# The last batch's sums for one product made a product earlier, and ten of VectorE's operations put into the states' tokens

## The chip, the cores and the metric

The kernel runs on one core of one Trainium2 chip. The metric is device time in microseconds. Five engines of the core appear in the profile: TensorE (PE for matmuls, PEld for the loading of the weights that a matmul holds fixed), VectorE (DVE), ScalarE (ACT), GpSimd (POOL) and SyncE (SP, which only issues DMAs here). Each engine works through its own instructions in the order in which the program writes them, and waits on semaphores for the others.

## What is computed

A cross attention between tokens and states, and then a feed-forward block on the tokens and the updated states. Everything is float32.

```python
B, H, S, Ns, D = 8, 8, 512, 32, 64          # d_model = H*D = 512, d_ff = 2048

scores = x @ state^T / sqrt(D)              # tokens read from states
a      = softmax(scores);   xread = a @ state
scores2 = state @ x^T / sqrt(D)             # states read from tokens
a2      = softmax(scores2); sread = a2 @ x
x = concat(xread, sread)                    # (8*544, 512)
h = x @ w_in                                # (4352, 2048)
g = h * sigmoid(1.702 * h)                  # "quick GELU"
out = g @ w_out                             # (4352, 512)
```

There are 8 batches of 512 tokens, and beside them 8 x 32 = 256 tokens that come from the states. The kernel treats these 256 as a last, smaller batch behind the eight.

## The kernel before

**Batches.** Batches 0 and 1 are begun in an order of their own while the weights arrive. From batch 1 on, one call of `strassen_two` (line 699) does the down projection `g @ w_out` of one batch, and the attention and the up projection of the next batch are threaded into it. The last call (batch 7) has no next batch of tokens: what is threaded into it is the preparation for the states' tokens. Then follow `up_strassen` (line 1046) for the states' up projection and `strassen` (line 549) for their down projection.

**Seven products in place of eight.** All these matrix products are done in Winograd's form of Strassen's method: both factors are cut into four quarters, sums of quarters are formed, seven products of half the size are made, and their results are added up. `strassen_two` does this with the whole down projection: its products are called P1, P2, P5, P6, P3, P7 and P4, in this order. P5, P6, P3, P7 and P4 are done by the same method once more (`lowly`, which calls `strassen_low`, line 660): each of them is seven small products of 4 x (128x128 by 128x128), which the profile shows as 8 matmuls and 8 weight loads. A small product accumulates in a PSUM bank (x, y or z), and VectorE adds the bank to what is kept (line 674). A bank that is used again for a further product must have been read first.

**The sums.** A left factor at the lower level needs four sums, each made by two VectorE operations 256 wide (line 727, `steps3` for P7, `steps4` for P4, `steps12` for P3). The sums for the right factors (weights) were made in batch 1 and are fetched from DRAM (`low_load`, line 618, and `low4_load`, line 637). One quarter of each weight matrix holds a difference in the place of the weight itself, for the lower level; `low_third` (line 656) is one 512-wide VectorE operation that turns it back. The states' down projection has one level only and needs the weights turned back: T1, T2, T3, T4 and B22.

**The states' up projection.** Its left factors are sums of the quarters of `w_in`. `sr_sums` lists twenty VectorE operations for them: 0 to 15 are 512 wide, eight for each half of the hidden units (0 to 7 the first half, 8 to 15 the second; in each half two operations each for the sums s1, s2, the difference kept in `w_in`, and s4), and 16 to 19 are 256 wide sums of the tokens. `up_strassen` then goes over four units u of hidden columns. Each unit has three groups: `begin` (products x and y), `middle` (z, x again, y again) and `end` (y and z for the last time), written in the order begin(u), end(u-1), middle(u). ScalarE copies or applies the GELU, VectorE adds (line 1074). Units 0 and 1 read the first half's sums, units 2 and 3 the second half's. The last `end`, and the sums of the down projection that go with it, are done inside `strassen`.

**The order of the work** is written out by hand. `hook(name)` is called behind products, and a dictionary says which functions are called there: "P3.4" is behind the fourth small product of P3, "run" lies between P3 and P7. The argument `own` of `lowly` does the same for the sums of the down projection itself; at one place `own` comes before the hook. In the last batch before the change, `steps3` is called between P3 and P7, and the order of the twenty operations is the table `order` near line 1269.

Of the kernel before, what the change touches and what calls it, by code (L numbers as in the profile page):

```python
# [20 lines left out]
def kernel(  # L21
# [32 lines left out]
    B, H, S, D = x.shape  # L54
    Ns = state.shape[2]
# [48 lines left out]
    T1, T2, T4 = (sums[:, i].rearrange("p (f n) -> p f n", f=HF) for i in range(3))  # L104
# [88 lines left out]
    for i, v in enumerate((8.0 * most, 8.0 * (most - least))):  # L193
        t = konst.tile([P, 1], FP32, name=f"edge_{i}")
# [410 lines left out]

    NU, QT = HF // 2, S // 2


    QF = HF // 2
    T3 = w_out[:, :HF, HN:]  # L610
    low_a, low_b = ([low[:, 3 * i + k].rearrange("p (f n) -> p f n", f=QF) for k in range(3)] for i in range(2))
# [87 lines left out]
    def strassen_two(key, dst, hooks, a4):  # L699
# [3 lines left out]
        B11, B21, B22 = w_out[:, :HF, :HN], w_out[:, HF:, :HN], w_out[:, HF:, HN:]  # L703
# [6 lines left out]
        def hook(name):  # L710
            for fn, args in hooks.get(name, ()):
                fn(*args)
# [74 lines left out]
        o, h0, h1 = low_banks()  # L787
# [6 lines left out]
        else:  # L794
# [9 lines left out]
            o, h0, h1 = low_banks()  # L804
# [24 lines left out]
        def lowly(name, left, right, kept, banks, R, own):  # L829
            def at(i):  # L830
                for fn in own.get(i, ()):
                    fn()
                hook(f"{name}.{i}")

            b11, t3, b21, b22 = halves_of(right)
            strassen_low(left, (b11, t3, b21, b22, *kept), banks, R, at)
# [4 lines left out]
        steps3, left3 = sums(y_of(0, half), (v1, v2, v4))  # L841
        steps4, left4 = sums(y_of(NU, half), (q1, q2, q4))
        own6 = {}
        if not plain:
            steps12, left12 = sums(y_of(NU, 0), r)
# [6 lines left out]
        if plain:  # L852
            for fn in steps3:
                fn()
            hook("P6")
            p3 = bank(3)
            product(p3, A_of(0, 1), B22, "P3")
            o, h0, h1 = low_banks()
            lowly("P7", left3, T3, low_b, [h0, h1, o], k3, {})
        else:  # L860
            hook("P6")
            p3 = o01
            o, h0, h1 = low_banks()
            lowly("P3", left12, B22, low_b, [h0, h1, o], p3, {1: steps12[2:3], 2: steps12[3:]})
            if key + 1 < B:
                low_load(5, 1)
            hook("run")
            for fn in steps3:
                fn()
            hook("T")  # L870
            o, h0, h1 = low_banks()
            lowly("P7", left3, T3, low_a, [o, h0, h1], k3, {k + 1: steps4[k : k + 1] for k in range(4)})
            if key + 1 < B:
                low_load(2, 0)
# [8 lines left out]
        if not plain:  # L883
            o, h0, h1 = low_banks()
# [68 lines left out]
    def up_sums(b):  # L953
# [6 lines left out]
        def rooms(step):  # L960
            if step == 0:
                t = apool.tile([P, NG, NB, Ns], FP32, tag="e1", name=f"ta_{b}").rearrange("p g i n -> p (g i n)")
                a["T"] = [t[:, QT * i : QT * (i + 1)] for i in range(4)]
            elif step == 1:
# [9 lines left out]
        def R(g, i):  # L974
            return lambda: a["aT"][:, g, QT * i : QT * (i + 1)]

# [66 lines left out]

        return steps, left, [each(v) for v in (r11, r21, r22, *ts)]

    def up_strassen(b, ntok, left, right, between=()):

        QT = ntok // 2
        b11, b21, b22, t1, t2, t3, t4 = right
        banks = {}  # L1050

        def product(u, bank, lhs, rhs, first):
            if first:
                if bank == "x":
                    banks[bank, u] = psH.tile([P, 2, QT], FP32, tag="h", name=f"upx_{b}_{u}")
                else:
                    o = bank_o[2 * (u % 2) + (bank == "z")]
                    banks[bank, u] = o[:, : 2 * QT].rearrange("p (k t) -> p k t", k=2)
            ps = banks[bank, u]
            n = len(lhs)  # L1060
            for k in range(2):
                o = 2 * P * (u % 2) + P * k
                for i in range(n):
                    nc.tensor.matmul(  # L1064
                        ps[:, k], lhs[i][:, o : o + P], rhs[i],
                        start=(first and k == 0 and i == 0), stop=(i == n - 1), skip_group_check=True,
                    )
            return ps

        def gelu(dst, src):  # L1070
            nc.scalar.activation(out=dst, in_=src, func=AF.Gelu_apprx_sigmoid)  # L1071

        def add(ps, x, dst):
            nc.vector.tensor_tensor(out=dst, in0=ps, in1=x, op=ALU.add)  # L1074


        def begin(u):
            l11, l12, l21, l22, m1, m2, m4 = left(u)
            G[b, u], G[b, NU + u] = free.pop(0), free.pop(0)
            _, c12 = quarters(b, u, ntok)  # L1080
            c21, _ = quarters(b, NU + u, ntok)
            nc.scalar.copy(c21, product(u, "x", l11, b11, True))
            add(product(u, "y", m2, t2, True), c21, c12)

        def middle(u):
            l11, l12, l21, l22, m1, m2, m4 = left(u)
            c11, c12 = quarters(b, u, ntok)
            c21, c22 = quarters(b, NU + u, ntok)
            z = product(u, "z", m1, t1, True)
            gelu(c11, product(u, "x", l12, b21, False))  # L1090
            add(product(u, "y", l21, t3, False), c21, c22)
            add(z, c22, c22)
            gelu(c22, c22)

        def end(u):
            l11, l12, l21, l22, m1, m2, m4 = left(u)
            c11, c12 = quarters(b, u, ntok)
            c21, c22 = quarters(b, NU + u, ntok)
            add(product(u, "y", l22, t4, False), c21, c21)
            gelu(c21, c21)  # L1100
            add(product(u, "z", m4, b22, False), c12, c12)
            gelu(c12, c12)
            if u:
                s12(b, u - 1, ntok)

        for u in range(NU):
            begin(u)
            if u:
                end(u - 1)
            middle(u)  # L1110
            for fn, args in between[u] if u in between else ():
                fn(*args)

        def rest():
            end(NU - 1)
            s12(b, NU - 1, ntok)
            for u in range(NU):
                s3(b, u, ntok)

        return rest  # L1120
# [84 lines left out]
    B11, B12, B21, B22 = (w_out[:, HF * i : HF * (i + 1), HN * k : HN * (k + 1)] for i in range(2) for k in range(2))  # L1205
# [41 lines left out]
    for b in range(1, B):  # L1247
        if b > 1:
            ahead = {"P1a": [(up_strassen(b, S, *parts_x(b), A[b]["sums"]), ())]}
            if b == 2:  # L1250
                ahead["P3.6"] = [(low_third, (T4,))]
        else:
            ahead = {
                "P1a": low_sums(T2, low_a)
                + [(low_keep, (2, turn_rooms[0])), (T_of, (T4, B21, T2)), (low_third, (T2,))],
                "P1b": low_sums(T3, low_b) + [(low_keep, (3, turn_rooms[1])), (low_third, (T3,))],
                "P4.7": low_sums(T1, low_b) + [(low_keep, (5, turn_rooms[1])), (low_third, (T1,)), (low_third, (B22,))],
            }
            for k, step in zip((4, 5, 6), low_sums(B22, low_a)):
                ahead[f"P7.{k}"] = [step]  # L1260
            ahead["P7.6"] += [(low_keep, (6, turn_rooms[0])), (low_load, (2, 0))]
        if b + 1 < B:
            if b > 1:
                turn_x(b + 1)
            hooks = hooks_next(b + 1)
        else:

            steps, left, right = sr_sums()
            order = (
                ("P5.6", 2), ("P6.1", 3), ("P6.2", 6), ("P6.3", 7), ("P6.4", 8), ("P3.3", 9), ("P3.4", 10), ("P3.5", 11),  # L1270
                ("P7.5", 12), ("P7.6", 13), ("P4.1", 16, 17), ("P4.5", 18, 19), ("P4.6", 14), ("P4.7", 15),
            )
            hooks = {name: [steps[i] for i in n] for name, *n in order}
            hooks["P3.6"] = [(low_third, (T1,))]
            hooks["P4.7"] += [(low_third, (t,)) for t in (T2, T3, T4, B22)]
            ahead["P1a"][:0] = [steps[i] for i in (0, 1, 4, 5)]
        for name, first in ahead.items():
            hooks[name] = first + hooks.get(name, [])
        a4 = {}

        at = hooks.setdefault("run" if b > 1 else "P3a", [])
        k = 3 if b + 1 < B else 0
        at[k:k] = [(low4_load if b > 1 else low4_make, (a4,))]
        strassen_two(b, out_of(b), hooks, a4 if b > 1 else None)
        if b + 2 < B:
            load_state(b + 2)
            load_x_squares(b + 2)
    nb = P // Ns
    strassen(
        "sr", B * Ns, lambda r, n: out_s[nb * r.start : nb * r.stop, :, n],  # L1290
        [[(up_strassen("sr", B * Ns, left, right), ())]],
    )


# [28 lines left out]
```

## Time and profile before

| quantity | value |
|---|---|
| median of 8 runs | 720.5 us (720.35 to 720.54) |
| profiled execution, its own time | 720.47 us |
| its span, first to last instruction | 718.7 us |
| mean granted TensorE clock | 0.999 |
| PE busy | 703.8 us |
| DVE busy | 586.6 us |
| ACT busy | 241.6 us |
| VectorE additions of line 1074 | 140, 88.1 us |
| P6 of the last batch begins (weights) | 636.15 us |
| P3, P7, P4 begin | 642.51, 648.81, 656.34 us |
| the states' up projection begins | 662.59 us |
| the states' down projection begins | 686.84 us |

Rows of the timeline give the start in us from the span's beginning, the duration in us, engine, line, operation, written tile and read tiles, shapes, and the count of equal instructions merged into the row; in brackets stands how long the engine had been idle and what ended that. A duration runs until the result has landed, so the next operation on an engine can start before it is over. "PEld" rows show when a product's weights begin to load, which is the clearest sign of when the product could start. In the list of waits a row gives who waited for whom, the sum in us, how often, and the longest.

### The profile page before, as it was taken

The numbers are of one execution on the slowest core, as the hardware profiler recorded it, in microseconds if no ns is written. First come the engines' busy times: TensorE is split into PE (matmuls) and PEld (weight loads), VectorE is DVE, ScalarE is ACT, GpSimd is POOL, SyncE is SP. The second block draws the span as 40 slices with busy tenths as digits, with TensorE's granted clock in tenths as the row PEclk, the third lists the DMA queues.
The fourth block names the chain that finished last, engine by engine and source line by source line (L and its number), as shares of the span: only waits on it lengthen the run. The fifth ranks groups of instructions, "written<-read, shape, count | busy, mean of one in ns | idle before, by whom it ended". The sixth has DMA issues, their size and how long they took to land.

```text
span 718.7 us, 12331 instructions
## 1 busy us (share of the span) xinstructions
PE 703.8 (98%) x4951; PEld 561.1 (78%) x4951; DVE 586.6 (82%) x1199; ACT 241.6 (34%) x467; POOL 0.8 (0%) x8
## 2 busy tenths in 40 slices
PE   7989999999999999999999999999999999999996
PEld 3433444467898799879998899889987998899995
DVE  6998899739868998699878986899789987989440
ACT  5686511024214422524233423342244215200210
POOL 0000000000000000000000000000000000000000
PEclk9999999999999999999999999999999999999999
DMA  8921246016154334405450445133432340031000
GB/s 229 363 89 55 92 148 149 2 59 160 46 176 62 59 106 162 77 1 123 156 122 0 111 141 133 18 74 125 154 50 53 110 162 15 1 115 62 17 1 29
DMA packets 104362, 68.43 MB, mean 95 GB/s; under 512 B 87665, under 2 KB 95345, under 8 KB 104305
## 3 DMA queue, kind: packets, MB, share of 16 engines
q1 hardware_dynamic: 104304, 67.65, 33.0%
q8 instruction: 39, 0.64, 0.4%
q14 instruction: 19, 0.15, 0.1%
HBM read 54.79 MB, written 12.85 MB: 94 GB/s over the span
## 4 chain that ended last, share of the span: by engine, by line
PE 88%; DVE 6%; DMA 3%; ACT 2%; issue 1%; SPq 0%; DVEq 0%; ACTq 0%
PE low L669 17%; PE o L1064 17%; PE o L720 14%; PE o L669 8%; PE o L518 7%; PE h L500 7%; PE upx L1064 6%; PE M L320 4%; PE o L561 2%; PE o L320 1%; PE sr L480 1%; PE warm L125 1%; DVE g L727 1%; DMA out_dram<-osb_sr 1%; PE eT L469 1%; DMA out_dram<-osb 1%
## 5 line engine op out<-in xcount | busy, mean ns | idle before, releaser
L1074 DVE TENSOR_TENSOR g<-o,g 128x512 f32<-128x512 f32 (+1 forms) x140 | 88.1, 650 | 55.5 <-PE o L1064 54.5
L720 PE MATMUL o<-w_out,g 128*128 128x256 f32 x480 | 107.9, 381 | 0.0
L720 PEld LDWEIGHTS o<-w_out,g 128*128 128x128 f32 x480 | 90.1, 190 | 18.4 <-issue 6.3
L1071 ACT ACTIVATE g<-g 128x512 f32<-128x512 f32 (+1 forms) x84 | 49.8, 600 | 101.9 <-DVE g L1074 101.9
L1064 PE MATMUL upx<-aT,M 128*128 128x256 f32 x192 | 49.3, 379 | 0.0
L1064 PE MATMUL o<-ta,M 128*128 128x256 f32 x192 | 49.3, 379 | 0.0
L1064 PE MATMUL o<-ta,ms 128*128 128x256 f32 x192 | 48.3, 379 | 0.0
L460 ACT COPY M<-M 128x512 f32<-128x512 f32 x64 | 33.2, 597 | 29.7 <-PE M L320 29.7
L1064 PEld LDWEIGHTS o<-ta,ms 128*128 128x128 f32 x192 | 36.5, 190 | 5.0
L1064 PEld LDWEIGHTS o<-ta,M 128*128 128x128 f32 x192 | 36.5, 190 | 5.0
L669 PE MATMUL low<-low,g 128*128 128x128 f32 x304 | 40.2, 275 | 0.0
L1064 PEld LDWEIGHTS upx<-aT,M 128*128 128x128 f32 x192 | 36.1, 190 | 4.7
L669 PEld LDWEIGHTS low<-low,g 128*128 128x128 f32 x304 | 37.0, 192 | 0.0
L669 PE MATMUL low<-sums,later 128*128 128x128 f32 x264 | 35.0, 276 | 0.1
L669 PEld LDWEIGHTS low<-sums,later 128*128 128x128 f32 x264 | 32.7, 192 | 0.7 <-DVE pu L674 0.3
L541 DVE TENSOR_TENSOR later<-g,g 128x512 f32<-128x512 f32 (+1 forms) x32 | 20.8, 650 | 14.9 <-ACT g L503 14.9
L320 PE MATMUL M<-w_in,stT 64*32 64x512 f32 x512 | 32.7, 594 | 0.2 <-ACT eT L470 0.2
L500 PE MATMUL h<-low,M 128*128 128x512 f32 x64 | 29.8, 600 | 1.5 <-DVE low L408 1.5
L500 PE MATMUL h<-aT,M 128*128 128x512 f32 x64 | 28.7, 599 | 1.4 <-ACT M L460 1.4
L518 PE MATMUL o<-w_out,g 128*128 128x512 f32 x64 | 28.7, 594 | 0.0
L669 PE MATMUL low<-w_out,g 128*128 128x128 f32 x216 | 28.5, 275 | 0.0
L518 PE MATMUL o<-w_out,sums 128*128 128x512 f32 x64 | 28.4, 594 | 0.0
(214 smaller groups left out, 1286.4 us busy)
## 6 DMA issues: line engine op xcount, KB each, us to landing
low<-low SPq DMA_DIRECT2D x34, 768.0 KB
later<-in_moe_w_out_dram SPq DMA_DIRECT2D x16, 512.0 KB
xn<-in_x_dram SPq DMA_DIRECT2D x28, 256.0 KB
w_out<-in_moe_w_in_dram SPq DMA_DIRECT2D x12, 512.0 KB
xsq<-in_x_dram SPq DMA_DIRECT2D x96, 64.0 KB
out_dram<-osb SPq DMA_DIRECT2D x18, 256.0 KB
out_dram<-later SPq DMA_DIRECT2D x14, 256.0 KB
later<-in_moe_w_in_dram SPq DMA_DIRECT2D x4, 512.0 KB
```

The costliest lines, as they stand in the source:

```text
L125: nc.tensor.matmul(ps, zeros[:, :P], zeros, start=True, stop=True)
L320: nc.tensor.matmul(ps[g][st], A[b]["stT"][rows, st], rhs(rows, j), start=True, stop=True)
L460: nc.scalar.copy(m[:, g], ps[g])
L500: nc.tensor.matmul(hps, lhs[i], rhs[i], start=(i == 0), stop=(i == n - 1))
L518: nc.tensor.matmul(ops, G[key, f // 2][:, f % 2, P * r : P * (r + 1)], w_out[:, f], start=(f == 0), stop=(f == NF - 1))
L541: nc.vector.tensor_tensor(out=s1, in0=a21, in1=a22, op=ALU.add)
L561: nc.tensor.matmul(ps[:, r], lhs[f][:, P * r : P * (r + 1)], rhs[:, f], start=(first and r == 0 and f == 0), stop=(f == HF - 1), skip_grou ...
L669: nc.tensor.matmul(ps, lhs[f], rhs[:, f], start=(first and f == 0), stop=(f == QF - 1), skip_group_check=True)
L720: nc.tensor.matmul(ps[:, r], lhs[f][:, P * r : P * (r + 1)], rhs[:, f], start=(r == 0 and f == 0), stop=(f == HF - 1), skip_group_check=True,)
L1064: nc.tensor.matmul(ps[:, k], lhs[i][:, o : o + P], rhs[i], start=(first and k == 0 and i == 0), stop=(i == n - 1), skip_group_check=True,)
L1071: nc.scalar.activation(out=dst, in_=src, func=AF.Gelu_apprx_sigmoid)
L1074: nc.vector.tensor_tensor(out=dst, in0=ps, in1=x, op=ALU.add)
```

## The change

In the last batch only, `steps3`, the sums for P7, is called within P3, one pair of operations behind each of its small products 3 to 6, and no longer between P3 and P7. Ten VectorE operations of 512 columns leave `strassen_two`: the operations 10 to 15 of `sr_sums` and the restorations of T2, T3, T4 and B22. They go into `up_strassen` as a list `beside`, from which the end of each group (`begin`, `middle`, `end`) takes one, behind the group's additions. Of the rest, operations 6 and 7 are called one hook later, 8 and 9 move from P6.4 and P3.3 to P7.5 and P7.6, and T1's restoration moves from behind P3's sixth small product to behind its seventh. The other batches are as before.

```diff
-            lowly("P3", left12, B22, low_b, [h0, h1, o], p3, {1: steps12[2:3], 2: steps12[3:]})
+            own3 = {1: steps12[2:3], 2: steps12[3:]}
+            if key + 1 == B:
+                own3.update({i + 3: steps3[i : i + 1] for i in range(4)})
+            lowly("P3", left12, B22, low_b, [h0, h1, o], p3, own3)
             if key + 1 < B:
                 low_load(5, 1)
             hook("run")
-            for fn in steps3:
-                fn()
+            if key + 1 < B:
+                for fn in steps3:
+                    fn()
             hook("T")
...
-    def up_strassen(b, ntok, left, right, between=()):
+    def up_strassen(b, ntok, left, right, between=(), beside=()):
+        beside = list(beside)
...
+        def aside():
+            if beside:
+                fn, args = beside.pop(0)
+                fn(*args)
...
         def begin(u):
...
             add(product(u, "y", m2, t2, True), c21, c12)
+            aside()
...
         def middle(u):
...
             gelu(c22, c22)
+            aside()
...
         def end(u):
...
             gelu(c12, c12)
+            aside()
             if u:
                 s12(b, u - 1, ntok)
...
             order = (
-                ("P5.6", 2), ("P6.1", 3), ("P6.2", 6), ("P6.3", 7), ("P6.4", 8), ("P3.3", 9), ("P3.4", 10), ("P3.5", 11),
-                ("P7.5", 12), ("P7.6", 13), ("P4.1", 16, 17), ("P4.5", 18, 19), ("P4.6", 14), ("P4.7", 15),
+                ("P5.6", 2), ("P6.1", 3), ("P6.3", 6), ("P6.4", 7), ("P7.5", 8), ("P7.6", 9), ("P4.1", 16, 17), ("P4.5", 18, 19),
             )
             hooks = {name: [steps[i] for i in n] for name, *n in order}
-            hooks["P3.6"] = [(low_third, (T1,))]
-            hooks["P4.7"] += [(low_third, (t,)) for t in (T2, T3, T4, B22)]
+            hooks["P3.7"] = [(low_third, (T1,))]
+            beside = steps[10:16] + [(low_third, (t,)) for t in (T2, T3, T4, B22)]
             ahead["P1a"][:0] = [steps[i] for i in (0, 1, 4, 5)]
...
-        [[(up_strassen("sr", B * Ns, left, right), ())]],
+        [[(up_strassen("sr", B * Ns, left, right, beside=beside), ())]],
```

## The prediction

> **What bounds the kernel now.** I read the page first: it says which engine carries the span and whether the clock is a topic.
>
> ```profile
> span 718.7 us, 12331 instructions
> ...
> PE 703.8 (98%) x4951; PEld 561.1 (78%) x4951; DVE 586.6 (82%) x1199; ACT 241.6 (34%) x467; POOL 0.8 (0%) x8
> ```
>
> TensorE (PE) is busy 98% of the span, and the page's row of the granted clock holds a 9 (90% or more) in each of its 40 slices. So an edit to VectorE (DVE) work pays only where TensorE is waiting for VectorE. The second view is therefore the list of waits, for TensorE alone, over the last batch and the states' tokens (625 to 720 us):
>
> ```profile
> PE o L1064 <- DVE g L1074: 0.8, 1, 0.8
> PE low L669 <- ACT pu L678: 0.5, 1, 0.5
> PE low L669 <- DVE later L674: 0.2, 1, 0.2
> ```
>
> Three waits, once each. The third view, the timeline around them, shows what VectorE was doing. First the seam from the low product P3 (with B22) to P7, then the start of the states' tokens:
>
> ```profile
> 648.81 0.97 PEld L669 LDWEIGHTS o<-w_out,g 128*128 128x128 f32 x8
> ...
> 649.33 0.75 DVE L727 TENSOR_TENSOR later<-g,g 128x256 f32<-128x256 f32 x2
> 650.00 0.75 DVE L727 TENSOR_TENSOR later<-later,g 128x256 f32<-128x256 f32 x2
> 650.06 0.27 ACT L678 COPY pu<-o 128x128 f32<-128x128 f32 x1 [4.29 <-PE o L669]
> 650.49 0.97 PEld L669 LDWEIGHTS low<-low,later 128*128 128x128 f32 x8 [0.70 <-ACT pu L678]
> ...
> 654.22 0.28 DVE L674 TENSOR_TENSOR later<-low,pu 128x128 f32<-128x128 f32 x1
> ...
> 654.56 0.97 PEld L669 LDWEIGHTS low<-w_out,later 128*128 128x128 f32 x8 [0.42 <-DVE later L674]
> ...
> 663.71 0.68 DVE L1208 TENSOR_TENSOR sums<-sums 128x512 f32<-128x512 f32 x1
> ...
> 665.52 0.69 DVE L1208 TENSOR_TENSOR w_out<-w_out 128x512 f32<-128x512 f32 x1
> 666.12 0.68 DVE L727 TENSOR_TENSOR later<-g,later 128x512 f32<-128x512 f32 x1
> ...
> 666.72 0.42 DVE L1074 TENSOR_TENSOR g<-o,g 128x256 f32<-128x256 f32 x1
> ...
> 667.19 0.97 PEld L1064 LDWEIGHTS o<-ta_sr,w_in 128*128 128x128 f32 x8 [0.95 <-DVE g L1074]
> ```
>
> A product here is 8 weight loads and 8 matmuls. P7's first needs no sums. Its second reads the sum made by the pair at 650.00: the first half of that pair ends at 650.42, the weights load at 650.49. The list names ScalarE's copy, but in P3 the like product loads at 643.40, before its copy at 643.76, so the copy is no condition. At 654.56 the sixth product waits for the addition of 654.22, late because VectorE was still making P7's and P4's sums. At 667.19 the states' second product on bank "y" (the fifth in all) waits for the addition of 666.72, which stood behind the four restorations of L1208 and the last sum of the output (L727).
>
> **How much is lost.** From 668.08 to 686.84 the weight loads of 21 successive products start 18.76 us apart: 0.893 us per product. From P6's first load (636.15) to 668.08 there are 33 products, 29.47 us at that pace, in 31.93 us: 2.46 us lost. By single steps: 0.79 at 650.49, 0.51 at 654.56, 1.03 at 667.19, 0.12 at 640.73 (P6) and 0.06 at 647.03 (P3); their sum, 2.51, agrees within 0.05.
>
> The Trainium skill, "Trainium Kernel Development and Optimization", Best Practices, says to judge TensorE by the busy share of its weight loads and not by its matmuls. By the matmul rows' idle times (0.54, 0.23, 0.76) the prize would be 1.5 us, by the weight loads' (0.70, 0.42, 0.95) 2.1 us. My sum goes by the pace, because that also counts products which are only stretched.
>
> **The change, part by part.** VectorE's prices, as start to start in a queue without gaps: 0.60 us for a 512-wide operation (663.71, 664.31, 664.91), 0.67 for a pair of 256-wide ones (649.33, 650.00), 0.20 for a 128-wide addition (648.29, 648.49), about 0.42 for a 256-wide addition from PSUM.
>
> *P6.* Steps 6 and 7 move one hook later and step 8 leaves: 0.60 less. The addition to "z" then ends near 640.4 instead of 640.67, before the sixth product's nominal 640.62. Gain 0.12.
>
> *P3.* Steps 9, 10 and 11 leave (1.80), T1's restoration moves from behind the sixth product to behind the seventh, and the four pairs of P7's sums (2.68) come in behind products 3 to 6. Walking the queue, 0.12 earlier than before: pair of hook 3 at 645.97, addition z 646.64 to 646.93, pair 646.84, addition y 647.51 to 647.80, pair 647.71, addition z 648.38 to 648.67, pair 648.58, last addition 649.25, T1's restoration 649.45 to 650.05. The sixth product wants the first of these by 646.86 and gets it at 646.98: 0.12 lost, against 0.06 before (a pair costs 0.07 more than the single operation it replaces). The seventh is ready at 647.85 against 647.87, and P7's first, which reuses the bank of the third addition, at 648.72 against 648.76: both just in time. This is the tightest place; 0.02 to 0.04 us are all the slack, so I bound it by 0.12 below and by four further 0.07 (0.4 in all) above, and take 0.12, because the pairs of 644.55 and 645.42 already ran beside P3's matmuls and the loads at the same 0.67.
>
> *P7.* Its sums are then ready before it starts: 0.79 is gone. P4's four pairs start behind T1's restoration, at 650.05, instead of 652.01; the sixth product's addition ends near 652.9, wanted at 653.24: 0.51 is gone. Steps 8 and 9 replace 12 and 13, the same size: nothing. What is late next would be a load: P7's second product reads sums of weights that SP fetches behind P6, and P4 the fetch behind it. Both issue at 642.8 and 643.2 and the DMA rows are empty from 649 us; after the change they are wanted at 649.7 and 655.9. The SP queue keeps its order; POOL has nothing here.
>
> *P4 and the handover.* Step 14, step 15 and the restorations of T2, T3, T4 and B22 leave: 6 x 0.60 = 3.6 us off the queue ahead of the output's last sum and of the first addition of the states' tokens. That addition then runs as soon as its product ends (1.2 us after the weights' start: 667.19, 668.39), 1 us before it is wanted: 1.03 is gone. The last output sum and its store on SP come some 4 us earlier, into DMA engines with little to do: nothing.
>
> *The ten operations behind the additions.* 10 x 0.60 = 6.0 us of VectorE, one behind each of the first ten groups. From 668 to 686 us VectorE is busy 7.88 of 18.00 and TensorE 18.00. A unit of seven products lasts 6.25 us; with three of these (1.8), five additions (2.1) and the sums of L541/L542 (0.8) VectorE has 4.7. Walked in order, the tightest: operation 11 ends 6.2 us after the stage's start, the next addition's product at 6.6; after that addition operation 12 delays the following one by 0.13, whose result only a GELU reads. An addition that a product waits for is done about 1 us early, so more than one 0.60 would have to stand ahead of it. Its data: steps 10 to 15 serve units 2 and 3 and are done by 13.9 us; unit 2's second product, the first reader, starts at 11.6 and needs 10 and 11 (6.2), its "m4" product at 19.6 needs 14 and 15. The restored weights are read after the four units' 25 us. Cost taken: 0; without that cover up to 6.0.
>
> *The end.* The last three stores hang on each other through one output buffer (3.45 us each), but the first starts with TensorE's product (addition at 706.26), and the store before it left 3 us earlier. So the tail moves with TensorE in full.
>
> Sum: 2.46 - 0.12 = 2.34 us. The profiled execution took 720.47 us (span 718.7 and 1.77 around it), 0.03 under the median 720.5: 718.13 on it, 718.15 on the median.
>
> **The rivals.**
> *P3 becomes VectorE's.* For: the slack of 0.02 to 0.04. Against: the same pairs beside the same matmuls. With 0.4 lost in P3 and another 0.3 passed on to P7, the gain is 1.7: 718.8. Chance 0.13.
>
> *The seam is not the sums'.* If P7's second product did wait for ScalarE's copy or for the fetch, 0.79 stays: gain 1.55, 718.95. If the handover's 1.03 stayed too: 720.0, no measurable difference. Against: the load at 643.40 ahead of its copy, the empty DMA rows. Chance 0.07, half of it with no difference.
>
> *Slower: the ten operations stand on TensorE's path in the states' tokens,* for instance because a sum written in one half of a room holds back a product that reads the other half. Price up to 6.0: 720.5 - 2.34 + 6.0 = 724.2. It decides from 0.23 us per operation, where it has eaten the 2.34. Against: in P7 the pairs of 652.01 and 652.88 wrote halves of g while products read the other halves at the 0.893 pace. Chance 0.05.
>
> *It does nothing:* the stretch is recovered and lost in the tail. Against: the tail's root is TensorE. With smaller losses of every sort adding to 1 us: 719.5. Chance 0.04.
>
> **How the numbers follow.** The forecast, 718.15, has 0.71; its own range is 717.9 (all 2.46, and 0.15 of spread) to 718.6. A measurement of this kernel tells about 0.2%, 1.44 us: faster means under 719.06. Faster: 0.71 + 0.13 + 0.035, less a little for P3 losing more = 0.86; same 0.08; slower 0.06. The range goes from 717.7 to 719.2, which takes in both faster rivals and leaves out the rest.
>
> **What would show it.** Right: no idle time before P7's second product or the states' fifth product; 636.15 to the product that was at 668.08 takes 29.6 us; L1208 and L1024 rows between the L1074 rows, with TensorE at 0.893 there. Wrong: gaps over 0.2 us ahead of P3's sixth or seventh product, or a wait of L1064 for L1024 or L1074.

## The result and the profile after

| | before | after |
|---|---|---|
| median | 720.51 us (28 runs, 720.32 to 720.86) | 718.16 us (10 runs, 717.98 to 718.28) |
| profiled execution | 720.47 us, span 718.7 | 718.06 us, span 716.3 |
| VectorE busy | 586.6 us | 586.9 us |

The ratio is 0.9967, with a 95% interval of 0.9959 to 0.9975: 2.35 us faster, where 718.15 had been forecast. VectorE does exactly the same work.

The head of the page for the changed kernel:

```profile
span 716.3 us, 12331 instructions
...
PE 703.3 (98%) x4951; PEld 560.9 (78%) x4951; DVE 586.9 (82%) x1199; ACT 241.8 (34%) x467; POOL 0.8 (0%) x8
```

The list of TensorE's waits over the same stretch, from 625 us to the end, had three rows before. Now nothing stands under its head:

```profile
core 0 of [0], span 716.3 us
engine line waited for: us in total, times, longest us
```

The timeline of the changed kernel, cut to the rows that answer to those of before. Line numbers have moved: L1064 is now L1071, L1074 is L1081, L1024 is L1029 and L1208 is L1223.

```profile
645.88 0.97 PEld L669 LDWEIGHTS low<-w_out,g 128*128 128x128 f32 x8
645.89 0.75 DVE L727 TENSOR_TENSOR later<-g,g 128x256 f32<-128x256 f32 x2
...
646.56 0.28 DVE L674 TENSOR_TENSOR later<-o,pu 128x128 f32<-128x128 f32 x1
646.76 0.75 DVE L727 TENSOR_TENSOR later<-later,g 128x256 f32<-128x256 f32 x2
646.89 0.97 PEld L669 LDWEIGHTS o<-w_out,spare_M 128*128 128x128 f32 x8
...
648.68 0.97 PEld L669 LDWEIGHTS o<-w_out,g 128*128 128x128 f32 x8
...
649.57 0.97 PEld L669 LDWEIGHTS low<-low,later 128*128 128x128 f32 x8
...
649.92 0.27 ACT L678 COPY pu<-o 128x128 f32<-128x128 f32 x1 [4.36 <-PE o L669]
...
661.89 0.69 DVE L727 TENSOR_TENSOR later<-g,later 128x512 f32<-128x512 f32 x1
...
663.35 0.42 DVE L1081 TENSOR_TENSOR g<-o,g 128x256 f32<-128x256 f32 x1 [0.77 <-PE o L1071]
663.69 0.68 DVE L1029 TENSOR_TENSOR ws<-ws,w_in 128x512 f32<-128x512 f32 x1
...
664.76 0.97 PEld L1071 LDWEIGHTS o<-ta_sr,w_in 128*128 128x128 f32 x8
```

The reader should see four things. The pairs of P7's sums (645.89, 646.76) lie between P3's additions. P7's second product loads at 649.57, one pace behind its first, and ahead of ScalarE's copy at 649.92: so it was the sums that it had waited for, and not the copy that the list of before named. The first addition of the states' tokens (663.35) now finds VectorE idle for 0.77 us, and one of the ten operations follows it. Their fifth product (664.76) no longer waits.

One loss is left: between the loads at 645.88 and 646.89 lie 1.01 us where the pace is 0.893. That is the 0.12 us of P3's sixth product. Every other of the 33 products from 636.05 to 665.65 starts within 0.02 us of the pace.

### The profile page after: what moved, and what is told of

The parts are those of the page before. It is cut to its first block, busy times and chain, and to the rows that moved or that the text cites. A ratio compares the mean times of both kernels' runs of the same rounds, so it can differ in the third digit from the quotient of the medians.

```text
span 716.3 us, 12331 instructions
## 1 busy us (share of the span) xinstructions
PE 703.3 (98%) x4951; PEld 560.9 (78%) x4951; DVE 586.9 (82%) x1199; ACT 241.8 (34%) x467; POOL 0.8 (0%) x8
## 4 chain that ended last, share of the span: by engine, by line
PE 90%; DVE 3%; DMA 3%; ACT 2%; issue 0%; SPq 0%; DVEq 0%; ACTq 0%
PE low L669 19%; PE o L1071 17%; PE o L720 14%; PE o L669 9%; PE o L518 7%; PE h L500 7%; PE upx L1071 6%; PE M L320 4%; PE o L561 2%; PE o L320 1%; PE sr L480 1%; PE warm L125 1%; PE upx_sr L1071 1%; DMA out_dram<-osb_sr 1%; PE eT L469 1%; DMA out_dram<-osb 1%
## 5 line engine op out<-in xcount | busy, mean ns | idle before, releaser
L1081 DVE TENSOR_TENSOR g<-o,g 128x512 f32<-128x512 f32 (+1 forms) x140 | 88.0, 650 | 51.4 <-PE o L1071 50.5
L1071 PE MATMUL upx<-aT,M 128*128 128x256 f32 x192 | 49.3, 379 | 0.0
L1071 PE MATMUL o<-ta,M 128*128 128x256 f32 x192 | 49.3, 379 | 0.0
L1071 PE MATMUL o<-ta,ms 128*128 128x256 f32 x192 | 48.3, 379 | 0.0
L1071 PEld LDWEIGHTS o<-ta,ms 128*128 128x128 f32 x192 | 36.5, 190 | 5.0
L1071 PEld LDWEIGHTS o<-ta,M 128*128 128x128 f32 x192 | 36.5, 190 | 5.0
L1071 PEld LDWEIGHTS upx<-aT,M 128*128 128x128 f32 x192 | 36.1, 190 | 4.7
```

The lines of the kernel that those rows point to most:

```text
L1071: nc.tensor.matmul(ps[:, k], lhs[i][:, o : o + P], rhs[i], start=(first and k == 0 and i == 0), stop=(i == n - 1), skip_group_check=True,)
```

## The experiments

In what follows "lost" is the distance between the starts of two products' weight loads less 0.893 us, the method of the prediction. The theory on trial is that TensorE loses time only where VectorE's queue, walked in order, delivers an addition or a sum late, and that the length of each delay can be had from the rows' durations.

### Each half alone

The first kernel keeps the sums within P3, and puts the ten operations back where they were:

```diff
-                ("P5.6", 2), ("P6.1", 3), ("P6.3", 6), ("P6.4", 7), ("P7.5", 8), ("P7.6", 9), ("P4.1", 16, 17), ("P4.5", 18, 19),
+                ("P5.6", 2), ("P6.1", 3), ("P6.2", 6), ("P6.3", 7), ("P6.4", 8), ("P3.3", 9), ("P3.4", 10), ("P3.5", 11),
+                ("P7.5", 12), ("P7.6", 13), ("P4.1", 16, 17), ("P4.5", 18, 19), ("P4.6", 14), ("P4.7", 15),
...
-            hooks["P3.7"] = [(low_third, (T1,))]
-            beside = steps[10:16] + [(low_third, (t,)) for t in (T2, T3, T4, B22)]
+            hooks["P3.6"] = [(low_third, (T1,))]
+            hooks["P4.7"] += [(low_third, (t,)) for t in (T2, T3, T4, B22)]
+            beside = ()
```

> The P3 half of the change alone: P7's sums within P3, all twenty preparing operations and the restorations where they were before. Theory of the queue (TensorE loses only where VectorE's queue, walked in order, is late): P3 now carries four pairs (4 x 0.67) on top of steps 9, 10, 11 and T1's restoration. Additions come late by 0.72 at the sixth product, 0.58 at the seventh and 0.58 at P7's first, 1.88 us in all, against 0.06 + 0.79 + 0.51 = 1.36 before; the handover's 1.03 stays. So slower than before by 0.5: 721.0. Rival, the parts simply add: the seam's 0.79 and 0.51 are saved whatever else stands in P3, 719.3.

Measured: 721.09 us (720.95 to 721.36) beside 720.48, ratio 1.0008 (1.0000 to 1.0017): slower by 0.61 us. The interval reaches down to 1.0000, but the fastest of the eleven executions (720.95) is slower than the slowest of the kernel before (720.81). Its timeline shows P3's sixth and seventh product and P7's first, each held by an addition:

```profile
647.33 0.28 DVE L674 TENSOR_TENSOR later<-o,pu 128x128 f32<-128x128 f32 x1
...
647.66 0.97 PEld L669 LDWEIGHTS o<-w_out,spare_M 128*128 128x128 f32 x8 [0.64 <-DVE later L674]
...
649.13 0.97 PEld L669 LDWEIGHTS low<-low,g 128*128 128x128 f32 x8 [0.50 <-DVE later L674]
...
650.60 0.97 PEld L669 LDWEIGHTS o<-w_out,g 128*128 128x128 f32 x8 [0.50 <-DVE later L674]
```

By the pace the losses are 0.73, 0.58 and 0.58, where 0.72, 0.58 and 0.58 had been worked out. One P3 lasts 6.25 us for TensorE, and VectorE cannot do P3's additions and sums, the two sums of the output at its head, the sums of P7 and steps 9 to 11 in that time. The last of the three late additions starts at 650.27 and T1's restoration behind it at 651.14, so these losses are not T1's.

The second kernel is the other half:

```diff
-            if key + 1 == B:
-                own3.update({i + 3: steps3[i : i + 1] for i in range(4)})
...
-            if key + 1 < B:
-                for fn in steps3:
-                    fn()
+            for fn in steps3:
+                fn()
...
-            hooks["P3.7"] = [(low_third, (T1,))]
+            hooks["P3.6"] = [(low_third, (T1,))]
```

> The other half alone: the ten operations behind the additions of the states' tokens, P7's sums between P3 and P7 as before, T1's restoration behind P3's sixth product as before. Theory of the queue: the handover's 1.03, P6's 0.12 and P3's 0.06 are gone; the seam keeps about 0.78 and 0.49, because the four pairs still start only behind P3's last addition, which waits for TensorE. Gain 1.2: 719.3. Rival, P3's relief by 1.8 us of VectorE lets the pairs start earlier and the seam closes too: 718.3. If the parts add, the two halves' gains sum to 2.35; by the queue they sum to about 0.7.

Measured: 719.30 us (719.16 to 719.38), ratio 0.9984 (0.9975 to 0.9993): faster by 1.18 us. The waits that are left are the two of the seam, which lose 0.78 and 0.50 by the pace:

```profile
PE low L669 <- ACT pu L678: 0.5, 1, 0.5
PE low L669 <- DVE later L674: 0.2, 1, 0.2
```

The relief in P3 did not reach the seam: P3's last addition waits for TensorE (648.90 in this kernel), and the four pairs stand behind it whatever VectorE had time for earlier. So the halves' effects are +0.61 and -1.18 us, together -0.57, and the whole change's is -2.35. The missing 1.78 us belongs to neither half: the sums fit into P3 only because the other half takes steps 9 to 11 out of it. One small part of the change is in neither kernel: both leave T1's restoration behind P3's sixth product, and no run shows what its move is worth alone.

### One operation more in P3

```diff
+            more = dict(out=later[:, 6], in0=sums[:, 0, :S], in1=sums[:, 0, S : 2 * S], op=ALU.subtract)
+            hooks["P3.3"] = [(lambda: nc.vector.tensor_tensor(**more), ())]
```

> As the changed kernel, with one more 512-wide VectorE operation (0.60 us, its result is not used) behind P3's third product. Theory of the queue: P3 has no slack left from its third product on, so the sixth product waits 0.72 in place of 0.12 and the rest of the queue shifts with it: 0.60 slower, 718.75. Rival, P3 has slack and the 0.12 comes from something else: 718.2.

Measured: 718.80 us (718.63 to 719.22), 0.64 above the changed kernel. The wait is where it was expected, ahead of the sixth product, and loses 0.73 us by the pace against 0.12:

```profile
646.82 0.69 DVE L1290 TENSOR_TENSOR later<-sums 128x512 f32<-128x512 f32 x1
647.42 0.28 DVE L674 TENSOR_TENSOR later<-o,pu 128x128 f32<-128x128 f32 x1
...
647.76 0.41 PEld L669 LDWEIGHTS o<-w_out,spare_M 128*128 128x128 f32 x3 [0.65 <-DVE later L674]
```

(The view ends at 648 us, so the last row holds only three of the product's eight loads.) So P3 is full. One more operation of 0.60 us there costs 0.61 by the pace.

### The place within the group

The diff puts each of the ten operations behind its group's additions. Here they stand ahead (shown for `begin`; `middle` and `end` likewise):

```diff
-            add(product(u, "y", m2, t2, True), c21, c12)
+            y = product(u, "y", m2, t2, True)
             aside()
+            add(y, c21, c12)
```

> As the changed kernel, but each of the ten operations stands ahead of its group's additions, not behind them. Theory of the queue: in the changed kernel's rows VectorE idles 0.36 to 1.66 us before most groups' first addition, and no product waits for an addition that is less than about 1 us early, so the place within the group is free: 718.2, and TensorE's pace of 0.893 us per product stays. Rival, the place behind the additions is what saves the time: every addition comes up to 0.60 later and TensorE waits; up to 6.0 slower, and more than 0.3 slower would speak for it.

Measured: 718.19 us (718.09 to 718.23) against 718.16, and TensorE has no wait from 625 us on. The rows show why: the operation runs in the time in which VectorE would have waited for the product.

```profile
662.61 0.69 DVE L1029 TENSOR_TENSOR ws<-ws,w_in 128x512 f32<-128x512 f32 x1
663.46 0.42 DVE L1081 TENSOR_TENSOR g<-o,g 128x256 f32<-128x256 f32 x1 [0.17 <-PE o L1071]
```

That the operations are in this stage matters; that they stand behind the additions does not, at this load.

### How much the states' tokens can carry

One, two or three further operations behind each of the ten (shown for one; `range(2)` and `range(3)` likewise):

```diff
         def aside():
             if beside:
                 fn, args = beside.pop(0)
                 fn(*args)
+                for _ in range(1):
+                    nc.vector.tensor_tensor(out=low[:, 0], in0=low[:, 1], in1=low[:, 2], op=ALU.subtract)
```

> As the changed kernel, with one further 512-wide VectorE operation (0.60 us, its result is not used) behind each of the ten moved ones: 6.0 us of VectorE more in the states' tokens. Theory of the queue, walked in order: no product gets its addition late, 718.2. Rival A, the states' tokens become VectorE's: three groups carry 3 x 1.2 + 2.1 + 0.8 = 6.5 us against TensorE's 6.25 per unit, some 0.25 for each of four units, 719.2. Rival B, the operations lie on TensorE's path: 724.2.

> As the changed kernel, with three further 512-wide operations behind each of the ten moved ones: 18 us of VectorE more. Theory of the queue: the cover is used up; walked in order the y products of the end groups wait 1.7 and 3.0 us and a begin group 0.5, 5.1 in the up projection, and about 2 more where the down projection meets the backlog: 725.3, between 723.3 and 726.5. Rival, an engine off the path costs nothing at any load: 718.2. Rival, all of it is on the path: 736.

One more: 718.10 us (718.02 to 718.22), no wait of TensorE. Rivals A and B fall. Around 675 us VectorE works without idle time, and still in time (L1088 is the further operation):

```profile
673.64 0.68 DVE L1088 TENSOR_TENSOR low<-low 128x512 f32<-128x512 f32 x1
674.24 0.42 DVE L1081 TENSOR_TENSOR g<-o,g 128x256 f32<-128x256 f32 x1
674.57 0.68 DVE L1029 TENSOR_TENSOR ws<-w_in,ws 128x512 f32<-128x512 f32 x1
675.17 0.68 DVE L1088 TENSOR_TENSOR low<-low 128x512 f32<-128x512 f32 x1
675.78 0.75 DVE L1081 TENSOR_TENSOR g<-o,g 128x256 f32<-128x256 f32 x2
```

Three more: 727.97 us (727.92 to 728.02), ratio 1.0104 (1.0089 to 1.0120), outside the 723.3 to 726.5 that the queue allowed. The timeline has the long waits where they were expected, ahead of the last y product of units 1 and 2:

```profile
676.66 1.47 PE L1071 MATMUL o<-ta_sr,w_in 128*128 128x128 f32 x8 [2.16 <-DVE g L1081]
...
687.21 1.74 PE L1071 MATMUL o<-ta_sr,w_in 128*128 128x128 f32 x8 [2.40 <-DVE g L1081]
```

The missing part is in the table of stretches (columns: stretch, its length, busy time of PE, PEld, DVE, ACT and POOL with the count of instructions, granted clock, DMA share, GB/s):

```profile
675.00:676.00 1.00, 0.00 (x0) 0.00 (x0) 0.97 (x2) 0.00 (x0) 0.00 (x0) 1.00 0.00 0
676.00:677.00 1.00, 0.34 (x3) 0.34 (x4) 0.97 (x4) 0.00 (x0) 0.00 (x0) 1.00 0.00 0
677.00:678.00 1.00, 1.00 (x9) 1.00 (x8) 1.00 (x3) 0.68 (x2) 0.00 (x0) 0.69 0.00 0
678.00:679.00 1.00, 1.00 (x7) 1.00 (x7) 0.96 (x2) 0.00 (x0) 0.00 (x0) 0.50 0.00 0
679.00:680.00 1.00, 1.00 (x6) 1.00 (x6) 0.97 (x3) 0.00 (x0) 0.00 (x0) 0.50 0.00 0
680.00:681.00 1.00, 1.00 (x8) 1.00 (x7) 1.00 (x3) 0.00 (x0) 0.00 (x0) 0.61 0.00 0
```

After each of the two waits the granted clock is 0.50 for about 3.4 us: worked out from the clocks of the last four stretches, 0.62, 1, 1 and 0.78 us of it lie in them, and after the second wait it lasts from 687.61 to 691.02. Sorted by the pace, the waits lose 0.45, 2.43, 2.67, 0.35 and, at the start of the down projection, 0.77: 6.67 us. The products at half clock lose 0.16, 0.82 and 0.66 after the first wait and 0.43, 0.82 and 0.38 after the second: 3.27 us. Together 9.94, and 727.97 lies 9.81 above the changed kernel. The queue theory's own part comes to 6.67 where 7.1 was expected, but not term by term: 5.55 us in the up projection for 5.1, and 1.12 at the down projection for about 2. Nor is it free of the clock, since VectorE works off its backlog while TensorE's products are slow. What the theory lacked altogether is a term for the clock.

To find where that begins, two more:

> As the changed kernel, with two further 512-wide operations behind each of the ten moved ones. With three further ones TensorE twice stood idle for 2.2 and 2.4 us, and the granted clock of the rows right after was 0.50 for some 3.3 us each time, 1.6 us lost on each; the queue theory had no such term and said 725.3 where 727.97 was measured. Walked again with the duration that those rows show (0.68 us per further operation), two further ones give one longer wait, about 2.1 us before the third unit's end group, a short one of 0.3, and about 0.7 at the down projection: 3.2 in all. If the clock holds over a wait of 2.1 us: 721.3. If it halves again: 1.6 more, 722.9.

Measured: a median of 721.78, but the ten executions differ far more than those of any other kernel here, and in step with the clock that each was granted on average:

```
mean granted clock   device time, us
0.998 to 1.000       720.91  720.94  720.96  721.13  721.46
0.995 to 0.997       722.10  722.13  722.17  722.26  723.02
```

The profiled execution is the one of 720.94. Its wait, in the timeline, is 1.85 us long:

```profile
682.35 1.16 PE L1071 MATMUL o<-ta_sr,w_in 128*128 128x128 f32 x8 [1.85 <-DVE g L1081]
```

and the clock of the stretch after it, the third number from the end in the table of stretches, is 1.00:

```profile
683.00:684.00 1.00, 1.00 (x11) 1.00 (x10) 0.96 (x3) 0.47 (x2) 0.00 (x0) 1.00 0.00 0
```

So the executions with the clock kept lie near the first expectation (721.3), and the others between it and the second (722.9), 1.2 us above the first group by the medians. That their clock fell after this same wait is likely, but was not seen in rows, because no such execution was profiled. The median of 721.78 lies between the two groups and describes neither.

### A further version

The walk of the queue names what makes P3's sixth product late: two sums of the output stand at P3's head. One of them, t01, is needed only in P4. And the end of the changed kernel, by its chain, is not TensorE's: the stores take turns in one buffer.

```profile
703.83 0.43 DVE osb_sr L580
704.27 0.02 issue
704.28 3.32 DMA out_dram<-osb_sr
...
707.72 0.44 DVE osb_sr L580
708.16 0.02 issue
708.18 3.30 DMA out_dram<-osb_sr
...
711.60 0.42 DVE osb_sr L580
```

```diff
-            o = opool.tile([P, nb, HN], FP32, tag="osb", name=f"osb_{key}_{i}{k}")
+            o = low[:, 2 * i + k, : nb * HN].rearrange("p (r n) -> p r n", r=nb)
...
-        tt(t01, p5, k2)
+        last = key + 1 == B
+        if not last:
+            tt(t01, p5, k2)
...
-            lowly("P7", left3, T3, low_a, [o, h0, h1], k3, {k + 1: steps4[k : k + 1] for k in range(4)})
+            lowly("P7", left3, T3, low_a, [o, h0, h1], k3, {k + 1: steps4[k : k + 1] for k in range(4)} | ({7: [lambda: tt(t01, p5, k2)]} if last else {}))
```

> As the changed kernel, with two further edits. The sum t01 of the last batch moves from ahead of P3 to behind P7's last product (0.72 us off the queue that makes P3's sixth product wait), and the states' four stores each get a room of their own in place of one buffer in turn. Theory: the 0.12 in P3 is gone, and the last addition, which in the changed kernel starts at 711.60 behind a store although TensorE is done at about 710.6, follows TensorE directly: 0.87 less. Together 1.0: 717.2. Rival, the last store takes as long as before because the stores share the DMA engines, not because they share a buffer: 718.0.

Measured: 717.13 us (717.03 to 717.25), ratio to before 0.9953 (0.9941 to 0.9966), 1.03 us under the changed kernel. The chain at the end is now TensorE's alone:

```profile
699.99 10.59 PE o L561 x49
710.58 0.02 issue
710.61 0.42 DVE low L580
```

The last addition starts 0.99 us earlier, so the rival, that the stores are held by the DMA engines and not by the buffer, falls. No product between P6 and the states' tokens loses more than 0.04 us by the pace any more, so P3's 0.12 is gone. It is the fastest kernel of this study.

## Why the prediction was right, point by point

**What bounds it.** Right. The list of waits is empty after, and the time that came back, 2.35 us, is that of TensorE's idle places. The prize taken from the pace (2.46, less 0.12) was nearer than the sums of idle times: 1.5 by the matmul rows, 2.1 by the weight loads. The Trainium skill's rule ("Trainium Kernel Development and Optimization", Best Practices) prefers the weight loads; that rule is about busy shares and was carried over to idle times here; of the two it gave the better value, still 0.3 us short of the 2.35 measured. That 718.15 met the measured 718.16 to 0.01 us is luck: 720.5 - 2.34 is 718.16 when it is written out, the single steps (2.51 less 0.12) would have given 718.11, and the medians of the kernel before, taken beside the different runs, differ by 0.09 (720.43 to 720.52).

**P6 and P3.** P6's 0.12 us is gone. P3's sixth product loses 0.12, as forecast, and the seventh and P7's first are just in time, as forecast. The absolute starts are 0.08 us earlier than worked out (addition at 646.56, forecast 646.64); P6, ahead of which nothing was changed, already begins 0.10 us earlier in this execution. The profiled execution of the changed kernel lies 0.10 under its median and that of the kernel before 0.04 under its own, so these two differ by 2.41 where the medians differ by 2.35. That P3 has hardly any slack, for which the prediction allowed up to 0.4 us of loss, the extra operation in P3 confirmed (+0.64). With 0.02 to 0.04 us to spare, the place could have gone either way.

**P7 and P4.** The losses of 0.79 and 0.51 are gone. The copy was no condition: 649.57 lies ahead of 649.92.

**The handover and the ten operations.** The 1.03 us is gone, and the output's last sum starts 4.2 us earlier (661.89, was 666.12), at no price. The ten operations cost nothing, as taken. The stated limit of the cover, that more than one 0.60 would have to stand ahead of an addition, was cautious: with a second one behind each, and ahead of the next addition, nothing is lost either. The "up to 6.0" for a lost cover was no real bound: it priced the operations' own time, and the run with eighteen more microseconds showed that a long wait is followed by products at half clock, for which the sum had no term.

**The end.** The tail moved with TensorE, as said. The reason given, that the first of the three stores starts with TensorE's product, holds; that the tail held another 0.9 us of its own was in the rows of before, and the prediction passed over it because the change did not touch it.

**The rivals.** "P3 becomes VectorE's" is what the first half alone does, so the mechanism is real, and the change escapes it by taking steps 9 to 11 out. "The seam is not the sums'" fell with the row at 649.57. "The ten operations stand on TensorE's path" fell with the two runs that move and double them; it comes true between two and three operations a group (0 us lost with two in all, about 2.8 with three where the clock was kept, 9.8 with four). "It does nothing" fell with the 2.35 us, whose ratio has an interval (0.9959 to 0.9975) that excludes 1.

## What to carry to other kernels

Price a reordering by walking the queue of the engine that delivers, operation by operation and start to start, against the pace of the engine that consumes; the seven medians forecast in this way, without the two that strained the clock, came within 0.1 us. Do not add up the parts of such a change: one half here costs 0.61 us alone and pays only because the other half makes room for it. And move work into the stage where the delivering engine idles before each delivery: its place within the group was free here.

## What was not expected of the hardware

Waits of TensorE of 2.16 and 2.40 us, each with several us at a granted clock of 1.00 right before it, were followed by about 3.4 us at 0.50, in all likelihood in each of the four executions timed (727.92 to 728.02, mean clock 0.994 or 0.995). A wait of 1.85 us left the clock alone in the execution that was profiled. The Trainium skill's page "TensorE: Matmul & The Clock Gate", section "What's actually happening", gives one idle window of about 3.4 us, free-running, as what halves the clock; the length of the slow phase here agrees with such a window, but the waits that brought it on were a third shorter. The two slow phases of this trace (677.37 to 680.79 and 687.61 to 691.02) begin 10.24 us apart, three times their own length of 3.41. That fits a fixed grid of such windows, on which one and the same wait would count or not by where it falls, as with the two groups of the kernel with two further operations; two phases of one trace are too few to show it.

An operation that reads and writes the same rooms as the one before it starts 0.71 to 0.73 us after it (the three further operations behind the first group start at 664.39, 665.10 and 665.83), where 512-wide operations on different rooms start 0.60 us apart. Which of the shared rooms holds it back was not tried.
